# Head selection of z: the second product of each pair at full array width

## The chip, the cores and the metric

The kernel runs on one core of a Trainium2 chip. Its time is the device time of one execution in microseconds (us). Of several runs the median is given. A trace of one profiled execution shows what each engine did: PE is TensorE (matrix products), PEld its weight loads, DVE VectorE, ACT ScalarE, POOL GpSimd, SP the engine that issues most DMAs.

## What is computed

Two linear-attention blocks, A and B, work on the same x (2048 rows of 640 features, 32 heads of 20 features each), and a gate mixes their outputs:

```python
def _A_ref(x, wqkv, wo):
    qkv = (x @ wqkv).reshape(B, S, 3, H, Dh).transpose(2, 0, 3, 1, 4)
    q, k, v = qkv[0], qkv[1], qkv[2]
    phi = lambda t: jnp.where(t > 0, t + 1, jnp.exp(t)) + 1e-6
    pq, pk = phi(q), phi(k)
    kv = jnp.einsum("bhsd,bhse->bhde", pk, v)
    z = jnp.einsum("bhsd->bhd", pk)
    num = jnp.einsum("bhqd,bhde->bhqe", pq, kv)
    den = jnp.einsum("bhqd,bhd->bhq", pq, z)[..., None] + 1e-6
    o = num / den
    return o.transpose(0, 2, 1, 3).reshape(B, S, D) @ wo
...
x = A_x
g = _sigmoid((x * gate_w).sum(-1, keepdims=True))
a = _A_ref(x, A_wqkv, A_wo)
b = _B_ref(x, B_wqkv, B_wo)
return g * a + (1 - g) * b
```

Block B is the same function with its own weights. Everything is bf16 outside the sums. The case is about `z`, the sum of phi(k) over all rows, and about the form in which it is handed to the product that gives the denominators.

## The kernel before

Products run on PE. Phi is made of an exponential on ACT and two operations on DVE. The large sums G (x transposed times phi(k)) and the last products are done by Strassen-like schemes with differences formed on DVE. Instructions are written in the order in which each engine executes them (`manual_schedule`), so an engine that waits holds up what is written behind it.

For each block the denominators are made in these steps:

- `z_rows` (L560 to L575) multiplies a matrix of ones with half-size sums of phi(k) that the Strassen scheme has anyway (`TK`). The ones are 32 columns wide, and four products lie side by side in four column groups of the array, so z arrives on all 128 rows of a PSUM tile `pt`, as four partial sums in four groups of 32 rows. There are 16 products of 320 columns (L566). A DVE multiply (L571) then takes z times the mask `E4` into the tile `zr`: row r (within its group of 32) keeps only the 20 features of head r, the others become zero. `E4` is built once at the start, on POOL (L184 to L191): ones, of which two `affine_select` per group keep feature f in row r if f // 20 is r.
- `z_pass` (L577 to L589) turns that round. For each of five remainders c, the features c, c + 5, c + 10 and so on (`mixed`, L330) are 128 columns of `zr`, five elements apart. A product with them as the stationary operand and `I4` as the moving operand (four identity matrices of 32 x 32, one below the other; L582) gives 128 features by 32 heads. The sums in `TK` give z for the right half of the features (heads 16 to 31), but left half minus right half for the left (heads 0 to 15). So the right half has to be added to the left: a second product (L583 and L584) takes the last 64 of the 128 columns of `zr`, which are the right half's, with columns 16 to 31 of `I4`, and adds them to rows 0 to 63, columns 0 to 15 of the first product's result. A DVE copy (L588) brings the five results to SBUF as `zsel`.
- `rec_pass` (L626) uses `zsel` as the stationary operand of 40 products with phi(q) (line L208 of the helper `by_group`, 32 columns wide in four column groups, tile `den`), takes the logarithm on ACT (L635), adds the gate on DVE (L639) and takes the exponential on ACT (L643). `norm_spread` (L679) spreads the reciprocals with eight products (L685) and copies them to `R` on ACT (L690), and `scale` (L695) multiplies phi(q) by `R` on DVE.

In block A, `z_rows` is called in `q_pass` (L811), behind the last product of q, and `z_pass` within `g_pass` (L847), ahead of its last four of 16 chunks (L467). `rec_pass` comes behind the first Strassen product (L526). In block B, `z_rows` and the first `p_diff` are called at L523 and L524, `z_pass` halfway through the second Strassen product (L527; products on line L496), and `rec_pass` at L533 behind three more `p_diff` (a DVE difference, L648). The load of `M[0]` from DRAM is issued at L521, and its first reader is a DVE sum (L545). `x_sum`, `k_sum`, `sq_sum` and `add_rows` are DVE sums (L648, L368).

`zr` lies in the pool `work` with one buffer, `E4` among the persistent tiles. Other products named below: `Masks` (L895, 120 and 40 columns of stationary operand), `kvt_mm` (L595, 80 columns), `m_half` (L620, 32 columns, spaced five elements apart, from `KVT`), `x_transpose` (L243, 128 columns).

Of the kernel before, what the change touches and what calls it, by code (L numbers as in the profile page):

```python
# [9 lines left out]
P = 128  # L10
FP32 = mybir.dt.float32
BF16 = mybir.dt.bfloat16
ACT = mybir.ActivationFunctionType
ALU = mybir.AluOpType

S, D, H = 2048, 640, 32
Dh = D // H
DT = D // P
# [4 lines left out]
HF = D // 2  # L23
# [11 lines left out]
def kernel(  # L35
# [11 lines left out]
    nc = tc.nc  # L47
# [4 lines left out]
    persist = ctx.enter_context(tc.tile_pool(name="persist", bufs=1))  # L52
    wpool = ctx.enter_context(tc.tile_pool(name="wpool", bufs=1))
    work = ctx.enter_context(tc.tile_pool(name="work", bufs=2))
# [28 lines left out]
    def ps(name, slot=None):  # L83

        return ps_raw(name, slot).bitcast(FP32).rearrange("p (b n) -> p b n", b=2)
# [8 lines left out]
    wo_sb = [None, None]  # L94
    ident = persist.tile([P, P], BF16, name="ident")
    I4 = persist.tile([P, H], BF16, name="I4")
    E4 = persist.tile([P, D], BF16, name="E4")
    maskE = persist.tile([P, K6], BF16, name="maskE")
    spread = persist.tile([P, P], BF16, name="spread")
    R = persist.tile([P, 2, 4, RB], BF16, name="R")  # L100
# [63 lines left out]
    for n in range(1, NB):  # L164
        for c in range(DT):
            nc.sync.dma_start_transpose(
                out=xT[:, c, n * HB:(n + 1) * HB], in_=x2[n * HB:(n + 1) * HB, c * P:(c + 1) * P]
# [4 lines left out]
    for r in range(4):  # L172
# [3 lines left out]
        out=spread[:].rearrange("p (h t) -> p h t", t=TW), in_=I4[:, :, None].to_broadcast([P, H, TW])  # L176
    )
    nc.gpsimd.memset(maskE[:], 1.0)
    for sign, base in ((1, 0), (-1, Dh - 1)):
        nc.gpsimd.affine_select(  # L180
            out=maskE[:], in_=maskE[:], pattern=[[-sign * Dh, K6 // Dh], [0, Dh]],
            compare_op=ALU.is_ge, fill=0.0, base=base, channel_multiplier=sign,
        )
    nc.gpsimd.memset(E4[:], 1.0)  # L184
    for r in range(4):
        rows = slice(32 * r, 32 * r + 32)
        for sign, base in ((1, 0), (-1, Dh - 1)):
            nc.gpsimd.affine_select(
                out=E4[rows], in_=E4[rows], pattern=[[sign, D]],
                compare_op=ALU.is_ge, fill=0.0, base=base, channel_multiplier=-sign * Dh,  # L190
# [139 lines left out]
    def mixed(t, m):  # L330

        return t[:, m::DT]
# [168 lines left out]
    def g_strassen(b, select, second, spare):  # L501
# [17 lines left out]
        if b == 1:  # L519
            m_block(5, 2)  # L520
            nc.sync.dma_start(out=M[0][:], in_=m_rows[:].rearrange("(p m) d -> p m d", m=DT))  # L521
            load_wo(1, nc.sync)
            zr = z_rows(1, 1)  # L523
            p_diff(part[0])  # L524
        else:
            rts = rec_pass(b, sel[0], 2)  # L526
        g_prod(odd, SX[2], TK[b][2], False, (lambda: sel.append(z_pass(1, zr))) if b == 1 else None)  # L527
        u2 = temp("u2")
        nc.scalar.copy(out=u2[:], in_=odd[:, :, 0:HF])
# [30 lines left out]
    def z_rows(b, slot=None):  # L560

        pt = ps(f"z{'AB'[b]}", slot)
        for hf in (1, 0):
            for k in range(hc // 4):
                for j in range(4):
                    nc.tensor.matmul(  # L566
                        pt[32 * j:32 * j + 32, hf, 0:HF], lhsT=ones[:], rhs=TK[b][4 - hf][:, 4 * k + j, :],
                        start=(k == 0), stop=(k == hc // 4 - 1), tile_position=(0, 32 * j),
                    )
        zr = work.tile([P, D], BF16, tag="zr", name="zr", bufs=1)  # L570
        nc.vector.tensor_tensor(  # L571
            out=zr[:].rearrange("p (b n) -> p b n", b=2), in0=pt[:, :, 0:HF],
            in1=E4[:].rearrange("p (b n) -> p b n", b=2), op=ALU.mult,
        )
        return pt, zr  # L575

    def z_pass(b, zr):  # L577

        pt, zr = zr
        for c in range(DT):  # L580
            at = HF + c * H
            nc.tensor.matmul(pt[:, 0, at:at + H], lhsT=mixed(zr[:], c), rhs=I4[:], start=True, stop=True)  # L582
            nc.tensor.matmul(  # L583
                pt[0:P // 2, 0, at:at + H // 2], lhsT=mixed(zr[:], c)[:, P // 2:P], rhs=I4[:, H // 2:H],  # L584
                start=False, stop=True, skip_group_check=True,
            )
        zsel = work.tile([P, DT, H], BF16, tag="zsel", name="zsel", bufs=1)
        nc.vector.tensor_copy(out=zsel[:], in_=pt[:, 0, HF:HF + DT * H].rearrange("p (c h) -> p c h", h=H))  # L588
        return zsel  # L589
# [209 lines left out]
    def q_pass(units):  # L799

        units = list(units)
        q_unit(0, *units.pop(0))
        for k in (2, 4):
            k_sum(0, k)
            q_unit(0, *units.pop(0), True)
            if k == 2:
                gate_spread()
        zs = []
        x_sum(1)
        q_unit(0, *units.pop(0), True)  # L810
        q_unit(0, *units.pop(0), True, behind=lambda: zs.append(z_rows(0)))  # L811
        zr = zs[0]
        sq_sum(4, 0)
        return zr
# [12 lines left out]
    for n in range(1, NB):  # L827
        nc.sync.dma_start(
            out=xn[:, n * CB:(n + 1) * CB, :], in_=x2[n * HB:(n + 1) * HB, :].rearrange("(q p) d -> p q d", p=P)
# [7 lines left out]
    with tc.manual_schedule():  # L837
# [6 lines left out]
        zr = q_pass([(m, 1) for m in range(DT)])  # L844
        wq[1] = load_w(1, "q", nc.sync)
        zsel = []
        g_pass(0, DT - 1, 3, lambda: zsel.append(z_pass(0, zr)), ST - CB)  # L847
        x_sum(2)
        x_sum(3)
# [152 lines left out]
        for i in range(1, half):  # L1002
            p, after = pairs[i], pairs[i + 1] if i + 1 < half else None
# [53 lines left out]
```

## Time and profile before

| | us |
|---|---|
| median of 3 runs (lowest, highest) | 190.41 (190.21, 190.52) |
| the profiled execution | 190.45 |
| its span, first to last instruction | 188.7 |
| PE busy | 183.9 |
| DVE busy | 149.2 |
| ACT busy | 90.1 |

The span is the part of the execution that the trace covers; 1.75 us lie outside. Matrix products are pipelined: a row's duration is that of one product from its start to its end, and the next starts long before, so a group's pace is read from the distance of starts. In the rows below, `128*64` means that the array tile has 128 rows and 64 columns, and `128x64` is the shape of the operand.

### The profile page before, as it was taken

Reading aid. Unit: us, or ns where it says so; the run is one execution under the profiler, and the core shown is the slowest. Engines: PE = TensorE matmul, PEld = TensorE weight load, DVE = VectorE, ACT = ScalarE, POOL = GpSimd, SP = SyncE. Lnnn points to the kernel's source line nnn. Section 1 sums busy time; section 2 is a strip of 40 time slices with the busy share of each in tenths; the row PEclk is TensorE's granted clock in tenths of the full one; section 3 lists DMA queues with packets and bytes.
Section 4 is the critical chain, followed back from the end, with each engine's and each line's share of the span. In section 5 each row is a group of like instructions: output and inputs, shape, how many; then the busy total and the mean of one; then the engine's idle time right before and its main releaser. Section 6 shows DMA issues by size and latency. Waiting matters only on the chain.

```text
span 188.7 us, 3594 instructions
## 1 busy us (share of the span) xinstructions
PE 183.9 (97%) x1426; PEld 123.9 (66%) x1434; DVE 149.2 (79%) x265; ACT 90.1 (48%) x159; POOL 9.1 (5%) x25
## 2 busy tenths in 40 slices
PE   8999999999999999999999999999999999999993
PEld 4666657755577677676666655757677776777772
DVE  1478867899979489997889897966797989787554
ACT  2065498548905532455777777672821611111110
POOL 8910000000000000000000000000000000000000
PEclk9999999999999999999999999999999999999999
DMA  6955449991540000006000000234800002311122
GB/s 182 326 126 78 109 92 339 312 225 65 136 152 0 0 3 0 0 3 174 0 0 2 3 0 0 61 104 157 207 0 0 3 0 90 122 69 70 41 104 70
DMA packets 19770, 16.18 MB, mean 86 GB/s; under 512 B 8969, under 2 KB 19625, under 8 KB 19753
## 3 DMA queue, kind: packets, MB, share of 16 engines
q1 hardware_dynamic: 18888, 15.13, 28.9%
q10 hardware_dynamic: 864, 0.82, 1.3%
q8 instruction: 11, 0.18, 0.4%
q14 instruction: 7, 0.05, 0.1%
HBM read 10.52 MB, written 3.46 MB: 74 GB/s over the span
## 4 chain that ended last, share of the span: by engine, by line
PE 94%; DVE 2%; ACT 1%; issue 1%; DVEq 0%; ACTq 0%
PE gs L496 17%; PE kA L283 12%; PE qA L335 11%; PE kB L283 11%; PE q L391 7%; PE ox L709 6%; PE oy L709 5%; PE oz L709 5%; PE ow L709 3%; PE gA L467 2%; PE gB L467 2%; PE warm L201 2%; PE qB L335 1%; PE q L335 1%; DVE osb L714 1%; PE kvA L895 1%
## 5 line engine op out<-in xcount | busy, mean ns | idle before, releaser
L283 PEld LDWEIGHTS <-xT 128*128 128x128 bf16 x320 | 31.0, 97 | 14.9 <-issue 0.5
L262 DVE TENSOR_SCALAR e<-e 128x640 bf16<-128x640 bf16 (+2 forms) x56 | 19.3, 345 | 7.3 <-ACT e L257 7.0
L283 PE MATMUL kB<-wkB,xT 128*128 128x320 bf16 x160 | 24.2, 299 | 0.0
L283 PE MATMUL kA<-wkA,xT 128*128 128x320 bf16 (+1 forms) x160 | 22.8, 299 | 0.3 <-ACT wkA L217 0.3
L335 PE MATMUL qA<-xT,wqA 128*128 128x512 bf16 x97 | 22.0, 379 | 0.2
L335 PEld LDWEIGHTS <-wqA 128*128 128x128 bf16 x100 | 11.7, 117 | 9.4
L496 PEld LDWEIGHTS <-xn 128*128 128x128 bf16 x128 | 12.3, 98 | 5.4 <-issue 0.9
L257 ACT ACTIVATE e<-kA 128x640 bf16<-128x640 f32 x16 | 11.2, 706 | 9.7 <-PE kA L283 9.6
L257 ACT ACTIVATE e<-kB 128x640 bf16<-128x640 f32 x16 | 11.3, 708 | 9.1 <-PE kB L283 8.9
L271 DVE SCALAR_TENSOR_TENSOR pk<-kA,e 128x640 bf16<-128x640 f32 x16 | 13.2, 825 | 2.6 <-DVE e L262 0.6
L271 DVE SCALAR_TENSOR_TENSOR pk<-kB,e 128x640 bf16<-128x640 f32 x16 | 13.2, 824 | 1.5
L753 ACT COPY u<-ox 128x320 f32<-128x320 f32 x8 | 3.4, 425 | 21.8 <-PE ox L709 21.8
L257 ACT ACTIVATE e<-q 128x512 bf16<-128x512 f32 x18 | 10.8, 597 | 5.4 <-PE q L391 3.8
L257 ACT ACTIVATE e<-qA 128x1024 bf16<-128x1024 f32 x10 | 10.2, 1021 | 5.1 <-PE qA L335 4.5
L709 PEld LDWEIGHTS <-xT 128*128 128x128 bf16 x85 | 8.0, 98 | 3.1 <-DVE xT L648 0.3
L709 PEld LDWEIGHTS <-pqTA 128*128 128x128 bf16 x85 | 7.9, 98 | 2.9 <-issue 0.2
L709 PEld LDWEIGHTS <-pqTB 128*128 128x128 bf16 x80 | 7.8, 98 | 3.0
L391 PE MATMUL q<-xT,wqB 128*128 128x512 bf16 x32 | 9.5, 379 | 0.0
L496 PE MATMUL gs<-pk,xn 128*128 128x320 bf16 x64 | 9.4, 299 | 0.0
L714 DVE TENSOR_TENSOR osb<-oz,u 128x320 bf16<-128x320 f32 (+1 forms) x18 | 8.0, 452 | 1.6 <-PE oz L709 0.9
L698 DVE TENSOR_TENSOR pqTA<-pqTA,R 128x2048 bf16<-128x2048 bf16 x5 | 5.8, 1219 | 3.2 <-ACT R L690 3.2
L737 ACT COPY p1s<-ox 128x320 f32<-128x320 f32 x8 | 3.4, 425 | 10.3 <-PE ox L709 10.3
(157 smaller groups left out, 320.0 us busy)
## 6 DMA issues: line engine op xcount, KB each, us to landing
out_dram<-osb SPq DMA_DIRECT2D x14, 160.0 KB, 1.9
xn<-in_A_x_dram SPq DMA_DIRECT2D x3, 640.0 KB, 5.6
wvA<-in_A_wqkv_dram SPq DMA_DIRECT2D x1, 800.0 KB
wkB<-in_B_wqkv_dram SPq DMA_DIRECT2D x1, 800.0 KB, 5.4
wqB<-in_B_wqkv_dram SPq DMA_DIRECT2D x1, 800.0 KB, 4.7
wvB<-in_B_wqkv_dram SPq DMA_DIRECT2D x1, 800.0 KB
MA<-m_rows SPq DMA_DIRECT2D x1, 800.0 KB, 4.6
woB<-in_B_wo_dram SPq DMA_DIRECT2D x1, 800.0 KB
```

Source lines behind the costliest of these rows:

```text
L201: nc.tensor.matmul(warm[:, 0, :], lhsT=one_l, rhs=one_r, start=True, stop=True)
L257: nc.scalar.activation(out=to, in_=part, func=ACT.Exp)
L262: nc.vector.tensor_scalar(self.e, self.e, 1.0, EPS, op0=ALU.min, op1=ALU.add)
L271: nc.vector.scalar_tensor_tensor(out=dst, in0=src, scalar=1.0 + EPS, in1=e, op0=ALU.add, op1=ALU.max)
L283: nc.tensor.matmul(pt[:, hf, 0:n], lhsT=xT[:, c, i * P:(i + 1) * P], rhs=wk[b][:, c, hf * HF:hf * HF + n], start=(c == 0), stop=(c == DT - 1),
L335: nc.tensor.matmul(dst, lhsT=mixed(wq[b][:, c, :], m), rhs=xT[:, c, n * HB:(n + 1) * HB], start=first, stop=last,)
L391: nc.tensor.matmul(dst, lhsT=left(c), rhs=right(c), start=first and k == 0, stop=k == len(cs) - 1, skip_group_check=not first,)
L467: nc.tensor.matmul(pt[:, hf, 0:HF], lhsT=xn[:, i, c * P:(c + 1) * P], rhs=pk[:, i, hf * HF:(hf + 1) * HF], start=(i == 0), stop=(i == ST - 1),
L496: nc.tensor.matmul(pt[:, n, 0:HF], lhsT=left[:, i, n * P:(n + 1) * P], rhs=right[:, i, :], start=(first and i == 0), stop=(i == hc - 1), s ...
L698: nc.vector.tensor_tensor(out=pqT[b][:, m, :], in0=pqT[b][:, m, :], in1=rec, op=ALU.mult)
L709: nc.tensor.matmul(dst, lhsT=left[:, c, r0:r0 + P], rhs=right[:, c, :], start=(first and c == 0), stop=(c == DT - 1), skip_group_check=not ...
L714: nc.vector.tensor_tensor(out=dst, in0=acc, in1=sb, op=ALU.add)
```

## The change

The mask and the selected sums become two halves of one persistent tile `zE` of 2 x 640 columns: the sums in the first half, `E4` in the second. `z_rows` writes the masked sums there and returns only the PSUM tile. In `z_pass` the second product of each pair takes 128 columns instead of 64: it starts at column 320 + c as before and, with the same step of five, reads on past column 640 into the mask. It writes all 128 rows of the result. The first 320 columns of `E4`, which it reads for rows 64 to 127, belong to heads 0 to 15 and hold ones only in rows 0 to 15 of each group. The moving operand is columns 16 to 31 of `I4`, which pick rows 16 to 31 of each group. So rows 64 to 127 get zero added.

```diff
-    E4 = persist.tile([P, D], BF16, name="E4")
+    zE = persist.tile([P, 2 * D], BF16, name="zE")
+    E4 = zE[:, D:2 * D]
...
-    nc.gpsimd.memset(E4[:], 1.0)
+    nc.gpsimd.memset(E4, 1.0)
...
-        zr = work.tile([P, D], BF16, tag="zr", name="zr", bufs=1)
         nc.vector.tensor_tensor(
-            out=zr[:].rearrange("p (b n) -> p b n", b=2), in0=pt[:, :, 0:HF],
-            in1=E4[:].rearrange("p (b n) -> p b n", b=2), op=ALU.mult,
+            out=zE[:, 0:D].rearrange("p (b n) -> p b n", b=2), in0=pt[:, :, 0:HF],
+            in1=E4.rearrange("p (b n) -> p b n", b=2), op=ALU.mult,
         )
-        return pt, zr
-
-    def z_pass(b, zr):
-
-        pt, zr = zr
+        return pt
+
+    def z_pass(b, pt):
+
         for c in range(DT):
             at = HF + c * H
-            nc.tensor.matmul(pt[:, 0, at:at + H], lhsT=mixed(zr[:], c), rhs=I4[:], start=True, stop=True)
+            nc.tensor.matmul(pt[:, 0, at:at + H], lhsT=zE[:, c:D:DT], rhs=I4[:], start=True, stop=True)
             nc.tensor.matmul(
-                pt[0:P // 2, 0, at:at + H // 2], lhsT=mixed(zr[:], c)[:, P // 2:P], rhs=I4[:, H // 2:H],
+                pt[:, 0, at:at + H // 2], lhsT=zE[:, HF + c:HF + D:DT], rhs=I4[:, H // 2:H],
                 start=False, stop=True, skip_group_check=True,
             )
```

## The prediction

> **What bounds the kernel now.** I read the page first: which engine is busy and which one the chain that ended last runs through. Then I asked the waits for those of TensorE (PE).
>
> ```profile
> PE 183.9 (97%) x1426; PEld 123.9 (66%) x1434; DVE 149.2 (79%) x265; ACT 90.1 (48%) x159; POOL 9.1 (5%) x25
> ...
> PE 94%; DVE 2%; ACT 1%; issue 1%; DVEq 0%; ACTq 0%
> ```
> ```profile
> PE warm L201 <- PEq L1041: 0.8, 1, 0.8
> PE kA L283 <- ACT wkA L217: 0.3, 1, 0.3
> ```
>
> PE is the bound: 97% busy, 94% of the chain, and its only two waits for others lie in the first 6 us. From there to the end it never waits for a vector engine or a transfer, so a microsecond that PE saves in its own stream moves everything behind it, unless a new wait appears.
>
> Next the chain, in order of time, around the first head selection (start, length, what):
>
> ```profile
> 50.35 3.37 PE gA L467 x24
> 53.72 0.02 PE zA L582
> 53.73 0.17 PE zA L583
> 53.90 0.14 PE zA L582
> ...
> 55.16 1.19 PE gA L467 x8
> 56.35 2.17 PE gs L496 x16
> ```
>
> All ten selection products lie on it, a pair of full and half product taking 0.14 + 0.17 = 0.31 us. The timeline gives their own starts: L582 begins at 53.55 and the next L467 at 55.09, that is 1.54 us for ten products; for the second block 127.47 to 129.00, 1.53 us. Together **3.07 us**. That is a lot: they move 32 and 16 columns. The rows of the tile zr and of two other groups say why (median durations, shapes of the stationary operand; in the timeline: start, length of the whole group, count):
>
> ```profile
> L582 PEld LDWEIGHTS <-zr x10: 117/118/118, 53.4 to 128.7; 128*128 128x128 bf16 x10
> L583 PEld LDWEIGHTS <-zr x10: 148/148/150, 53.7 to 128.8; 128*64 128x64 bf16 x10
> ...
> L583 PE MATMUL zA<-I,zr x5: 239/239/240, 53.7 to 54.9; 128*64 128x16 bf16 x5
> ```
> ```profile
> 142.71 0.93 PE L595 MATMUL mid<-GT,wvB 128*80 128x80 bf16 x20
> ```
> ```profile
> 82.85 0.71 PE L895 MATMUL kvA<-GT,wvA 128*120 128x120 bf16 x10
> ```
> ```profile
> 84.59 0.30 PE L895 MATMUL kvA<-GT,wvA 128*40 128x40 bf16 x5
> ```
>
> In the L595 group each product has its own weights, and they start (0.93 - 0.207) / 19 = 0.038 us apart (0.207 is the duration of one); in the 120-column group (0.71 - 0.218) / 9 = 0.055; in the 40-column group (0.30 - 0.18) / 4 = 0.03 by rounded figures. So different weights at every product do not cost 0.14 to 0.17 us. In the timeline the weight loads of L595 start while the product before is running; those of L583 start at 53.66, 53.98 and so on, together with their own product, after the full product before is nearly through. The same hole stands wherever the column width of the array tile changes: the timeline shows it as idle time of PEld "issue" (0.41 us before the 32-column L566 loads, 0.26 us behind them, 0.26 us ahead of L208). It does not stand between 128 and 120 columns (82.63 to 82.85 is one ordinary 0.22 us step) nor between 128 and 80. I read this as: **going between the full-width array and a 64-column or narrower tile lets the running product drain first**, and the z passes do it ten times each.
>
> **The change, part by part.**
>
> 1. The ten half products become full ones: 128 columns of stationary operand instead of 64, 16 moving columns as before, written to all 128 rows. Same count of instructions, no DMA, nothing moved in any queue. The added 64 columns are E4's first 64 for that remainder, whose rows with heads 16 to 31 are zero, and I4's columns 16 to 31 pick just those rows: zeros are added. What changes is the step from one product to the next. Every load is now like L582's: 128 columns, five elements apart, 117 ns. The trace has no stream of such loads behind short products, so I bound the step from the nearest rows. From below: 0.025 us (the 40-column group: loads of 97 ns; behind the first, its exact starts lie 25 ns apart). From above: 0.055 us (the 120-column group, loads of 135 ns, so longer than 117). Between them lies L595, whose loads take 117 ns at its start and 123 ns later, at 0.038 us. That row is nearest to 117 ns, and I take **0.038 us**.
>
>    After: 10 x 0.038 = 0.38 us a pass in place of 1.535, a gain of 1.155; two passes, **2.31 us**. With 0.025: 2.57. With 0.055: 1.97.
>
> 2. The first products behind each pass: today the L467 load at 55.09 starts with its product, an entry cost inside the 1.54 us, already counted. No further gain.
>
> 3. zr leaves the work pool, E4 becomes the upper half of zE; the DVE multiply (L571, 817 and 824 ns) reads and writes the same shapes. Cost nothing: it is the same instruction, and its write for block B would wait for readers that ended at 55 us, 71 us before. The products now read E4, written by POOL, whose work ends in the first three of the page's 40 slices. Tiles between the two pools sit 1,280 bytes elsewhere; no row prices that, I take nothing, and the range has room for 0.2 us.
>
> Now what could become late when PE arrives 1.15 us earlier. **Block A**: zsel's cast (L588, 0.33 us) waited 0.90 us for the last half product; it will start at about 54.3, when the SQ sum ends on DVE, and end near 54.6, while denA (L208, now 58.45) then comes at 57.3. The sum SX2 (55.44 to 56.66) moves up with DVE to about 55.8, wanted at 59.66 - 1.15 = 58.5. The reciprocals end at 61.53 less 0.9, wanted at 64.12 - 1.15 = 63.0. **Block B**: zsel waited 1.06 us; the p_diff ahead of it on DVE ends at 128.04, the products will end at about 127.47 + 9 x 0.038 + 0.18 = 128.0, so the cast ends near 128.4; denB is wanted at 130.19 - 1.15 = 129.0. The Ln, add and Exp behind it (131.52 to 133.27) hang on denB and move with it, for the last p_diff, ending at 131.64, moves up 1.06 as well; the add had waited 0.39 us for ACT. One thing does not move: the load of M[0] from DRAM, issued at 128.77 with 4.6 us to landing, so 133.4. The DVE sum on it (0.98 us from 134.14) would be ready at 133.0, waits some 0.4 us and ends at 134.4; next on DVE is the scaling, which starts with R at 136.34 - 1.15 = 135.2. So 0.8 us of cover is left; without it the 0.4 us would fall on the scaling, not at once on PE.
>
> **Sum.** Span 188.7 - 2.31 = 186.4 us; this execution took 190.45, 1.75 outside the span, and the median of the runs is 190.41, 0.04 below it. I predict 190.41 - 2.31 = **188.1 us**, with its own range 187.8 to 188.5.
>
> **The rivals.**
>
> *A, the wide load costs by its columns (chance 6%).* Loads of scattered columns seem to cost by width: 148 ns for 64 columns, 117 for the 32-column loads of KVT, about 1 ns a column. If the new operand were loaded at that rate, its load took 93 ns more than L582's, the step 0.131, a pass 5 x (0.131 + 0.038) = 0.85, the gain 2 x 0.69 = 1.37: 189.0 us. Against it: L582 loads 128 scattered columns in 117 ns, less than 64 take, and the new operand has the same count and spacing.
> The Trainium skill, "TensorE: Matmul & The Clock Gate", section "LDWEIGHTS (loading the stationary operand)", puts a load at columns / 1.2 ns, which would be 107 ns for each of the ten and, as an estimate by that page, 2 x (1.535 - 1.07) = 0.93 us gained, 189.5 us. The trace speaks against it as a step: 128-column loads of L243 stand behind products that start 0.055 us apart.
>
> *B, a pass's gain is swallowed by a wait (4%).* In block B the reciprocals are ready only 0.41 us before L685 (133.27 against 133.68). If zsel or a p_diff came so late that this stayed where it is, the 1.16 us of that pass would be lost: 189.25 us. Against it: each link hangs on the one before and starts earlier, as worked out above.
>
> *C, the change doesn't do what it says (6%).* The hole might come from short products with scattered weights in themselves, not from the width. Then each step stays near the 0.14 us now seen from full to half: 10 x 0.14 = 1.40, gain 0.13 a pass, 190.1 us. For it: no row has scattered 128-column loads back to back behind short products. Against it: the L595 step, and the holes at L566 and L208, whose products are long.
>
> *D, slower (4%).* The added product accumulates into columns that the full product just wrote, now in all rows. If it, and the product behind it, had to wait until its forerunner is through (212 ns, the duration of L582), ten steps made 2.12 us, 0.59 a pass lost, 191.6 us. It turns to a loss from a step of 0.154 us on. Against it: the five 40-column products accumulate into the same columns and start some 0.03 us apart.
>
> **How the numbers follow.** 80% for the forecast, and A 6, B 4, C 6, D 4. A change of 0.2% (0.38 us) is about what can be told from none, so faster means below 190.03: forecast, A and B, 0.90; C is within it, 0.06; D slower, 0.04. The range: the forecast's own 187.8 to 188.5, with 0.2 us for places in memory below, and above it up to 188.9, where a step between 0.055 and A's would lie: 187.6 to 188.9.
>
> **What would show it.** Right: L583's stationary rows read 128x128 at about 117 ns; the next L467 and L496 start about 0.38 us behind the first selection product; the DVE waits of 0.90 and 1.06 us ahead of zsel go; PE has no new wait. Wrong: starts still 0.14 us apart (C), loads near 210 ns (A), an idle PE ahead of L208 or L685 (B), or starts 0.2 us apart (D).

## The result and the profile after

The changed kernel takes **188.49 us** in the median of 6 runs (187.96 to 188.76), the kernel before 190.47 in 6 runs beside it (190.21 to 190.74). The ratio is 0.989, with a 95% interval of 0.9872 to 0.9908. The profiled execution took 187.96 us, with a span of 186.2 us where it had been 188.7.

First the page of the changed kernel: busy time, and the chain that ended last.

```profile
PE 181.7 (98%) x1434; PEld 121.6 (65%) x1434; DVE 149.1 (80%) x265; ACT 90.2 (48%) x159; POOL 9.1 (5%) x25
...
PE 92%; DVE 3%; DMA 2%; ACT 1%; issue 0%; SPq 0%; DVEq 0%; ACTq 0%
```

PE's busy time went down by 2.2 us and that of its weight loader by 2.3; that of the other engines moved by 0.1 at most, and PE is the bound as before. The 2% of DMA in the chain are a load of weights (wkA) that PE waited for at the start. (Eight more product records than before are no change in the program: a few were missing in the first trace.) The chain around the first selection, in order of time (start, length, what):

```profile
53.59 0.02 PE zA L581
53.61 0.03 PE zA L582
53.64 0.05 PE zA L581
...
53.95 1.10 PE gA L468 x8
```

A pair takes 0.08 us now, where it took 0.31. The rows of the tile zE say how the two kinds of product changed:

```profile
L581 PEld LDWEIGHTS <-zE x10: 117/128/130, 53.3 to 126.4; 128*128 128x128 bf16 x10
L582 PEld LDWEIGHTS <-zE x10: 117/128/130, 53.4 to 126.5; 128*128 128x128 bf16 x10
...
L582 PE MATMUL zA<-I,zE x5: 182/183/184, 53.5 to 53.8; 128*128 128x16 bf16 x5
```

The second product's load fell from 148 to 128 ns although it has twice the columns, and the product itself from 239 to 183 ns. The first product's load rose from 117 to 128 ns, with an operand of the same form: a load's duration also depends on what stands beside it. Last the waits, first PE's and then one of DVE's behind the second selection:

```profile
PE warm L202 <- PEq L1040: 0.8, 1, 0.8
PE kA L284 <- ACT wkA L218: 0.3, 1, 0.3
PE kA L284 <- DMA wkA<-in_A_wqkv_dram: 0.2, 1, 0.2
```
```profile
131.91 0.99 DVE L647 TENSOR_TENSOR TM<-MA 128x1600 bf16<-128x1600 bf16 x1 [0.17 <-DMA MA<-m_rows]
133.86 2.36 DVE L697 TENSOR_TENSOR pqTB<-pqTB,R 128x2048 bf16<-128x2048 bf16 x2 [0.96 <-ACT R L689]
```

PE's waits still all lie in the first 6 us. The waits of DVE ahead of zsel (0.90 and 1.06 us) are gone. A new one of 0.17 us stands ahead of the sum on M[0], and 0.96 us of idle time behind it absorb it.

### The profile page after: what moved, and what is told of

It is laid out like the page before. It is cut to its first block, busy times and chain, and to the rows that moved or that the text cites. A ratio compares the mean times of both kernels' runs of the same rounds, so it can differ in the third digit from the quotient of the medians.

```text
span 186.2 us, 3602 instructions
## 1 busy us (share of the span) xinstructions
PE 181.7 (98%) x1434; PEld 121.6 (65%) x1434; DVE 149.1 (80%) x265; ACT 90.2 (48%) x159; POOL 9.1 (5%) x25
## 4 chain that ended last, share of the span: by engine, by line
PE 92%; DVE 3%; DMA 2%; ACT 1%; issue 0%; SPq 0%; DVEq 0%; ACTq 0%
PE gs L497 17%; PE kA L284 12%; PE qA L336 12%; PE kB L284 11%; PE q L392 7%; PE ox L708 6%; PE oy L708 5%; PE oz L708 5%; PE ow L708 3%; PE gB L468 2%; PE gA L468 2%; DMA wkA<-in_A_wqkv_dram 2%; PE qB L336 1%; PE q L336 1%; DVE osb L713 1%; PE kvA L894 1%
```

## The experiments

Theory: the running product drains wherever the column width of the array tile changes, and that hole, not the load or the product, was what the half products cost. Ten runs follow: the changed kernel again (e1), eight different edits, and one of them a second time (e10).

The table puts all of them side by side. Each set of runs had the kernel before beside it (190.46 us for e1 to e4, 190.67 for e5 to e8, 190.47 for e9 and e10), and each ratio is to that. The passes are from the start of the first selection product to the start of the product behind the last one, taken from the starts in each trace; "ahead" is the start of the first selection product, "between" the stretch from the end of pass A to the start of pass B, "behind" that from pass B to the end.

| kernel | ahead | pass A | between | pass B | behind | median (range) |
|---|---|---|---|---|---|---|
| before | 53.56 | 1.535 | 72.38 | 1.537 | 59.71 | 190.47 (190.21-190.74) |
| changed | 53.43 | 0.378 | 72.35 | 0.378 | 59.68 | 188.49 (187.96-188.76) |
| e1 changed, again | 53.59 | 0.378 | 72.36 | 0.379 | 59.68 | 188.09 (187.87-188.44) |
| e2 layout, 64 columns | 53.83 | 1.544 | 72.37 | 1.544 | 59.69 | 190.69 (190.29-190.97) |
| e3 65 columns | 54.28 | 0.511 | 72.36 | 0.507 | 59.68 | 188.60 (188.17-189.06) |
| e4 grouped | 53.35 | 0.743 | 72.36 | 0.742 | 59.69 | 189.19 (188.60-189.45) |
| e5 96 columns | 53.58 | 0.681 | 72.35 | 0.677 | 59.68 | 189.18 (188.49-189.97) |
| e6 all 64 columns | 53.93 | 0.861 | 72.46 | 0.860 | 59.71 | 189.53 (189.22-189.85) |
| e7 first product twice | 53.95 | 0.579 | 72.34 | 0.577 | 59.68 | 188.72 (188.41-188.84) |
| e8 contiguous | 53.69 | 0.255 | 72.36 | 0.256 | 59.68 | 187.93 (187.88-188.20) |
| e9 contiguous, Masks | 54.22 | 0.256 | 72.19 | 0.253 | 59.67 | 188.09 (187.62-188.47) |
| e10 contiguous, again | 54.04 | 0.255 | 72.36 | 0.255 | 59.68 | 187.82 (187.81-188.30) |

**e1, the changed kernel again.**

> The changed kernel once more, to size the gain and its spread. The trace of its first execution gave 0.38 us for each pass of ten products (before 1.54 and 1.53), so 2.31 us less by the sum and 2.5 us less span. Theory: the median lies 2.3 us below the kernel before, 188.1 to 188.2. Rival: some of the gain is given back in most executions, at a place that the one profiled did not show; then the median is again near 188.5 and profiles of it show a wait or a late transfer that was not there before.

188.09 us, ratio 0.9876 (0.986 to 0.9892). "Between" and "behind" are those of the kernel before to 0.03 us, so nothing is given back in what follows the passes. What differs from execution to execution is "ahead": 53.35 to 54.28 us over the twelve traces, in products that none of the edits touches. Its place is the first 10 us: from the start of kA's 21st product (at 8.64 us in the changed kernel, 9.48 in e3) to the first selection product it is 44.8 to 44.9 us in all twelve. PE's timeline in e3, the latest:

```profile
3.78 1.27 PE L244 MATMUL xt<-ident,xn 128*128 128x128 bf16 x10
...
7.06 0.44 PE L244 MATMUL xt<-ident,xn 128*128 128x128 bf16 x5
```

and in the changed kernel's first profile:

```profile
3.85 0.73 PE L244 MATMUL xt<-ident,xn 128*128 128x128 bf16 x10
...
6.43 0.44 PE L244 MATMUL xt<-ident,xn 128*128 128x128 bf16 x5
```

The same ten transposes take 1.27 or 0.73 us: they start 107 ns apart in e3 and, after a first step of 67, 55 to 56 ns apart in the changed kernel; the later five start 55 to 56 ns apart in both. A pace half as fast gives way to the full one at a different moment. The traces' own record of the granted clock shows that moment: it begins, with full clock, at 6.52 us in e3 and at 3.80 in the changed kernel. Ten of the twelve traces have such a record; it begins between 3.8 and 6.8 us, and the later it begins, the later the selection starts, but for two pairs of neighbours. One of the two is e3's: its chain runs through a load of wkA that lands at 9.17 us, just ahead of a product of kA at 9.21, and this costs about 0.2 us of its own. The Trainium skill, "TensorE: Matmul & The Clock Gate", section "Part 1: The HAM clock gate", says that PE starts at half its clock and is let go by a window that runs free of the kernel; these rows agree. The scatter of the two medians of one kernel (188.49 and 188.09) has the size of this start (0.93 us over the traces); that it is the whole of it was not shown run by run, since only one execution of each has a trace.

**e2, one part undone.** The tile zE stays, the second product is half again:

```diff
-                pt[:, 0, at:at + H // 2], lhsT=zE[:, HF + c:HF + D:DT], rhs=I4[:, H // 2:H],
+                pt[0:P // 2, 0, at:at + H // 2], lhsT=zE[:, HF + c:D:DT], rhs=I4[:, H // 2:H],
```

> Undoes one part: sums and mask lie side by side as in the changed kernel, but the second product takes 64 columns and writes 64 rows again. Theory (the running product drains wherever the column width of the array tile changes): starts 0.14 and 0.17 us apart again, 1.54 us a pass, 190.4 us. Rival (places in memory made the gain): near 188.5 us.

190.69 us, ratio 1.0011 (1.0001 to 1.0021); 1.544 us a pass. The gain goes completely, so the places in memory had no part in it.

**e3, 65 columns.**

```diff
-                pt[:, 0, at:at + H // 2], lhsT=zE[:, HF + c:HF + D:DT], rhs=I4[:, H // 2:H],
+                pt[0:65, 0, at:at + H // 2], lhsT=zE[:, HF + c:HF + c + 64 * DT + 1:DT], rhs=I4[:, H // 2:H],
```

> The second product takes 65 columns instead of 128 or 64, one column into the mask, and writes 65 rows. Theory (drain at a change between the full-width tile and a 64-column tile): 65 columns no longer fit the half tile, so the hole is gone and only the load remains, about 1 ns a column: a load near 149 ns, steps 0.07 and 0.04 us, a pair 0.11, a pass 0.54, 0.3 us over the changed kernel, about 188.8 us. Rival (any scattered load of fewer than 128 columns makes the hole): steps as with 64 columns, 1.5 us a pass, 190.4 us.

188.60 us, ratio 0.9898 (0.9882 to 0.9914); a pass of 0.511 us against 0.54 expected. This run decides. A pair in the chain and the load in e3:

```profile
54.46 0.07 PE zA L582
54.53 0.03 PE zA L581
```
```profile
L582 PEld LDWEIGHTS <-zE x10: 150/152/155, 54.3 to 127.6; 128*65 128x65 bf16 x10
```

and a pair in e2:

```profile
54.01 0.17 PE zA L582
54.18 0.14 PE zA L581
```

One more column, with the load as long as ever (152 ns, where 64 columns took 148 to 151): the pair falls from 0.31 to 0.10 us. So the length of the load does not make the hole; the step over 64 columns does away with it. Two changes of width cost 0.313 - 0.102 = 0.21 us. The Trainium skill, "TensorEngine Tiling (Array Packing)", section "Key Properties", says that a change of the tiling mode drains TensorE; the trace agrees, and these 0.21 us are what going to the 64-column tile and back costs here.

**e4, two changes a pass instead of ten.** The five full products of the kernel before first, then its five half ones:

```diff
         for c in range(DT):
             at = HF + c * H
-            nc.tensor.matmul(pt[:, 0, at:at + H], lhsT=mixed(zr[:], c), rhs=I4[:], start=True, stop=True)
+            nc.tensor.matmul(
+                pt[:, 0, at:at + H], lhsT=mixed(zr[:], c), rhs=I4[:], start=(c == 0), stop=True,
+                skip_group_check=(c > 0),
+            )
+        for c in range(DT):
+            at = HF + c * H
```

> The kernel before, but with its five full products first and then its five half products, so that the tile's width changes twice a pass and not ten times. Theory (drain at the change): 4 x 0.038 + 0.14 + 4 x 0.07 + 0.17 = 0.74 us a pass, 0.79 us less than before, about 188.9 us. Rival (each half product brings its hole with it): 1.5 us a pass, 190.4 us.

189.19 us, ratio 0.9929 (0.9913 to 0.9945). The chain shows the pass in two pieces:

```profile
53.51 0.17 PE zA L582 x5
53.68 0.47 PE zA L588 x5
54.16 1.19 PE gA L467 x8
```

0.743 us a pass against 0.74 expected. The same products in another order are 0.79 us a pass cheaper, so the hole belongs to the change, not to the half product. Against e3's 0.511 without any change the pass is 0.23 longer; that holds the two changes and the other order of the loads, which the run does not part.

**e5, 96 columns** (the edit of e3 with 96 in place of 65).

> The second product takes 96 columns. Theory (no hole at this width, a load of about 1 ns a scattered column unless there are 128): a load near 180 ns, steps 0.10 and 0.04 us, a pass 0.70, 0.6 us over the changed kernel, about 189.1 us. Rival (the load costs the same for every count above 64): a pass of 0.38 us, as the changed kernel.

0.68 us a pass, 189.18 us, ratio 0.9924 (0.9901 to 0.9946). The loads in e5:

```profile
L581 PEld LDWEIGHTS <-zE x10: 117/182/183, 53.5 to 127.0; 128*128 128x128 bf16 x10
L582 PEld LDWEIGHTS <-zE x10: 185/186/188, 53.6 to 127.2; 128*96 128x96 bf16 x10
```

No hole, but pairs of 0.136 us, where 65 columns made 0.102 and 128 columns 0.078: between 65 and 96, scattered columns cost about 1.1 ns each (34 ns for 31 more), and 128 cost less than either. The pairs say this, not the loads' durations: the full-width loads (L581), with 128 ns in the changed kernel, read 182 ns here, beside the slow ones.

**e6, all in 64-column tiles.**

```diff
-            nc.tensor.matmul(pt[:, 0, at:at + H], lhsT=mixed(zr[:], c), rhs=I4[:], start=True, stop=True)
+            for k in range(2):
+                nc.tensor.matmul(
+                    pt[64 * k:64 * k + 64, 0, at:at + H], lhsT=mixed(zr[:], c)[:, 64 * k:64 * k + 64], rhs=I4[:],
+                    start=True, stop=True, tile_position=(0, 64 * k),
+                )
             nc.tensor.matmul(
-                pt[0:P // 2, 0, at:at + H // 2], lhsT=mixed(zr[:], c)[:, P // 2:P], rhs=I4[:, H // 2:H],
-                start=False, stop=True, skip_group_check=True,
+                pt[0:64, 0, at:at + H // 2], lhsT=mixed(zr[:], c)[:, P // 2:P], rhs=I4[:, H // 2:H],
+                start=False, stop=True, skip_group_check=True, tile_position=(0, 0),
```

> All products in 64-column tiles: each full product is cut into two of 64 columns, one for each half of the array, and the added one stays as before, 15 products a pass and no change of width inside it. Theory (the change costs, not the width): a hole at the way in and out (0.14 and 0.17 us) and at most 0.07 us a step between, 1.3 us a pass if the two halves work in turn, 1.0 if side by side; 189.3 to 189.9 us. Rival (each 64-column product brings its hole): 15 x 0.14 = 2.1 us a pass, 191.5 us.

189.53 us, ratio 0.9944 (0.9929 to 0.9959). Fifteen products in 64-column tiles take 0.86 us, less than ten of mixed width took (1.54). The hole on the way in lies ahead of the first start and so outside this count: that product starts 0.23 us behind the one before it, where the other kernels have 0.14. With these 0.09 it is 0.95 us, near the 1.0 expected for two halves side by side; the two halves often start 3 to 7 ns apart. A narrow tile alone is no loss of that size; the changes are.

**e7, a doubled cost.** Each first product of the changed kernel is issued twice.

> The changed kernel with each first product written twice (the same result once more), 15 full products a pass. Theory: a full product with scattered weights costs its load alone, 0.039 us: 0.58 us a pass, 0.39 us over the changed kernel. Rival (the products were covered by something else, so PE's pace is not what sets the end): no change in time.

0.58 us a pass as expected, 0.040 us for each product more; 188.72 us, ratio 0.9899 (0.9883 to 0.9915). Its profiled execution took 0.75 us more than that of e1 (188.84 and 188.09): 0.40 lies in the two passes and 0.36 ahead of them, in the start.

**e8, contiguous loads.** The sums and the mask are kept remainder by remainder; the multiply reads PSUM in that order:

```diff
-    zE = persist.tile([P, 2 * D], BF16, name="zE")
-    E4 = zE[:, D:2 * D]
+    zE = persist.tile([P, DT, 2 * P], BF16, name="zE")
+    E4 = zE[:, :, P:2 * P]
...
-                out=E4[rows], in_=E4[rows], pattern=[[sign, D]],
+                out=E4[rows], in_=E4[rows], pattern=[[sign, DT], [sign * DT, P]],
...
-            out=zE[:, 0:D].rearrange("p (b n) -> p b n", b=2), in0=pt[:, :, 0:HF],
-            in1=E4.rearrange("p (b n) -> p b n", b=2), op=ALU.mult,
+            out=zE[:, :, 0:P].rearrange("p c (b j) -> p c b j", b=2),
+            in0=pt[:, :, 0:HF].rearrange("p b (j c) -> p c b j", c=DT),
+            in1=E4.rearrange("p c (b j) -> p c b j", b=2), op=ALU.mult,
...
-            nc.tensor.matmul(pt[:, 0, at:at + H], lhsT=zE[:, c:D:DT], rhs=I4[:], start=True, stop=True)
+            nc.tensor.matmul(pt[:, 0, at:at + H], lhsT=zE[:, c, 0:P], rhs=I4[:], start=True, stop=True)
...
-                pt[:, 0, at:at + H // 2], lhsT=zE[:, HF + c:HF + D:DT], rhs=I4[:, H // 2:H],
+                pt[:, 0, at:at + H // 2], lhsT=zE[:, c, 64:64 + P], rhs=I4[:, H // 2:H],
```

> The changed kernel with the columns of each remainder side by side in memory: the multiply writes sums in that order (it reads PSUM with a step of five), the mask is built in it, and all ten stationary operands are contiguous. Theory (the step of 0.039 us is the scattered load): loads of 97 ns and steps near 0.026 us, 0.26 us a pass, 0.25 us less than the changed kernel. Rival (the step has another bound): still 0.039. A second thing that could go wrong: the multiply gets longer than 0.82 us by its reads; in block B it ended 0.06 us before the first weight load, so PE would wait there for what is over.

187.93 us, ratio 0.9863 (0.9848 to 0.9878). The first products' loads (the second ones' have the same numbers) and the multiply in e8:

```profile
L582 PEld LDWEIGHTS <-zE x10: 95/96/98, 53.6 to 126.5; 128*128 128x128 bf16 x10
```
```profile
125.33 0.82 DVE L571 TENSOR_TENSOR zE<-zB,zE 128x640 bf16<-128x640 f32 x1 [1.62 <-PE zB L567]
```

Loads of 96 ns instead of 128, ten products in 0.255 us, 0.12 us a pass less; the multiply is no longer for its scattered reads (0.82 us). So the step of 0.039 us was the scattered load. What bounds the 0.025 us that are left, the load or something else, no run shows. The median lies below the changed kernel's, but 0.25 us is less than the start moves it, so the passes are the proof, not the medians.

**e9 and e10, the same cause at another place.** The last five products of Masks (40 columns) read on to 72 columns, beside e8's kernel again. The tile of v's weights gets 32 zeros (`WIDE`) behind its end for it:

```diff
+                            wide = max(n, 40 + WIDE)
                             nc.tensor.matmul(
-                                self.pt[:n, g // 4, at + f0 - g * K6:at + f1 - g * K6],
-                                lhsT=wv[0][:, c, g * K6:g * K6 + n],
+                                self.pt[:wide, g // 4, at + f0 - g * K6:at + f1 - g * K6],
+                                lhsT=wv_flat[0][:, c * D + g * K6:c * D + g * K6 + wide],
```

> The kernel with contiguous selection operands, and the same edit at another place: the last five products of Masks (40 columns of the weights of v, which make the tile change to 64 columns and back) read on to 72 columns, into the next row of the weights or, for the last, into 32 zeros behind them; rows 40 to 71 of the result are not used. In the trace of before the 377 ns from the last 120-column product to the product behind the block hold a step of 148 and one of 112 ns. Theory (drain at a change of width): 0.055 and five steps near 0.035 us, so 0.23 us, 0.15 us less than the kernel without this edit, to be seen in the profile rather than in the median. Rival (the holes there are of another kind): still 0.38 us.

> The kernel with contiguous selection operands once more, beside the one above on the same chip: 0.15 us over it by the theory, and the steps of its selection products 25 ns again; its median 187.9 to 188.4, as the start of the execution falls.

PE's timeline at Masks in e9, then in e10:

```profile
82.22 1.97 PE L905 MATMUL kvA<-GT,wvA 128*120 128x120 bf16 x35
84.03 0.38 PE L394 MATMUL q<-SQ,MB 128*128 128x512 bf16 x1
```
```profile
82.04 2.04 PE L895 MATMUL kvA<-GT,wvA 128*120 128x120 bf16 x35
84.01 0.39 PE L392 MATMUL q<-SQ,MB 128*128 128x512 bf16 x1
```

From the first of these products to the one behind them 1.81 us against 1.97, and "between" is 0.17 us shorter: the 0.15 expected. The medians (188.09 and 187.82, ratios 0.9855, interval 0.9824 to 0.9886, and 0.9853, 0.9827 to 0.988) do not tell the two kernels apart; e9's trace starts its selection 0.18 us later. e10's median lies 0.08 us below the 187.9 to 188.4 expected.

## Why the prediction was right

- **What bounds the kernel.** Right: PE sets the end. "Between" and "behind" stay the same to 0.03 us, so each microsecond taken out of a pass came out of the span.
- **The cause.** Right, and now shown rather than read: e3 (one column), e4 (the order) and e6 (the width alone) each part the change of width from the load and from the half product. That the hole is the running product draining is still a reading: the runs show to what it belongs and what it costs, and the ends of products in a trace are modelled.
- **The size.** A step of 0.038 us was taken, between 0.025 and 0.055; the traces have 0.038 to 0.040, and 0.378 us a pass against 0.38. The sum of 2.31 us became 2.32 in the two passes. Both of its parts are visible now: about 1.02 us a pass are holes (1.535 - 0.511), and 0.13 (0.511 - 0.378) is the quick load of 128 columns against the slow one of 65. The bound from below, 0.025, was not idle either: e8 reaches it with contiguous loads. That 0.038 came so close is in part luck. L595 was picked because its loads take 117 ns, as L582's did; in the changed kernel these take 128 ns, between L595's 123 (0.038) and the 135 of the 120-column group (0.055). By load length the step would have come out near 0.045 us and the gain near 2.17 (an estimate from these rows), and e5 shows that load lengths are no sure guide.
- **The time.** The profiled execution lost 2.5 us of span: 2.32 in the passes, 0.12 in its start, 0.05 in the rest. By the medians the gain is 1.98 us in the first set and 2.37 in e1's, on either side of 2.31. The median of 188.49 lies 0.4 above the predicted 188.1, inside the forecast's own range by 0.01 us only; that it did not fall outside owes something to where the starts fell. The start was not in the sum, as one profile cannot show its scatter.
- **What moved and what did not.** The selection sums, denominators and reciprocals moved up with PE as worked out. The load of M[0] did make DVE wait, 0.17 us where 0.4 was expected, and the scaling behind it kept 0.96 us of cover; in e1's trace it was 0.43 and 0.70. The loads of the selection, expected to stay at about 117 ns, take 128.
- **The rivals.** A (a wide load costs by its columns) fell: a pair with 96 columns took 0.136 us, with 128 columns 0.078. B fell: PE has no new wait behind the passes (the one for wkA, 0.2 us, lies in the start). C fell with the steps of 0.039 us and with e2. D fell: full products that add into columns just written start 0.028 to 0.040 us behind those that wrote them.

## What to carry to other kernels

Where PE sets the end, look for products whose stationary operand has 64 columns or fewer among full-width ones: each switch there and back cost 0.21 us here, about five quick products. Reading on into columns that multiply by zero, or into rows of the result that nobody reads, takes the holes away without a further product; putting the narrow products together leaves two of them. After that the steps went by the operand that is loaded: of full-width operands, one laid out contiguously took 25 ns a step, one of every fifth column 39.

## What the runs showed of the hardware

Steps between short products, each with its own weights, by operand: contiguous, 40 columns 25 ns, 72 columns 35 ns (e9), 120 columns 55 ns, but 128 columns 25 ns (e8); ten bytes apart (every fifth column), 64 columns 76 ns in a row of such products (e4), 128 columns 39 ns. In turn with full-width ones, the step behind a product of 65 columns was about 76 ns (e3) and behind one of 96 columns 110 (e5), and the step ahead of it 25. A narrower operand can be the slower one. And the first 10 us differ by up to 0.93 us between executions, for the most part as PE comes to full pace at a different moment. The profile page's row of the granted clock does not show this: it reads full speed from the first slice on, also where the trace has no record of the clock yet.
